# Four small memsets from GpSimd to VectorE, and one load from SyncE to ScalarE, at the start of an attention and gated FFN kernel

## The chip, the cores and the metric

The kernel runs on one core of a Trainium2 chip. The metric is the device time of one execution in microseconds (us), as the median of several executions. Engines are named as the profile names them: PE is TensorE (PEld its weight loads), DVE is VectorE, ACT is ScalarE, POOL is GpSimd, SP is SyncE. A load that GpSimd issues goes through DMA queue q0 (software_dynamic in the profile), one that SyncE or ScalarE issues through a hardware_dynamic queue (q1 for SyncE in this trace).

## The reference, cut to what matters

Attention over 8 batches with 8 heads, in which keys and values are first projected from 1024 positions to 64 by two small matrices E and F, followed by a gated feed-forward network over 8192 tokens.

```python
# q, k, v: (8, 8, 1024, 64); E, F: (64, 1024); w_gate, w_val: (512, 1536); w_out: (1536, 512)
k_proj = np.einsum('ks,bhsd->bhkd', E, k)
v_proj = np.einsum('ks,bhsd->bhkd', F, v)
scores = scale * np.matmul(q, k_proj.transpose(0, 1, 3, 2))
attn = softmax(scores)                       # written out in the reference
x = np.matmul(attn, v_proj)                  # -> (8192, 512) tokens
gate = 1.0 / (1.0 + np.exp(-(x @ w_gate)))
out = gate * (x @ w_val) @ w_out
```

So nothing can be projected before E, F and the first keys are on the chip, and nothing of the feed-forward network can start before a first block of attention is done.

## The kernel before: the parts that the change and the steps touch

The kernel is a list of operations; each is added with the keys it reads and writes, and waits between engines follow from these. Each engine runs its own operations in the order of the list. The parts that matter stand at its start.

```python
def pool(fn, r=(), w=()):
    return add("POOL", fn, r=r, w=w)

def load(o, i, w, sem, r=(), tie=()):        # every load of k, q, v and weights: issued by GpSimd
    add("POOL", lambda e: e.dma_start(o, i), r=r, w=w, dma=sem, t=26.0, tie=tie)

def start_loads():
    for src, rows, n in ((E, slice(0, 64), "E"), (F, slice(64, 128), "F")):
        add("SP", lambda e, src=src, rows=rows: e.dma_start(EF[rows, :], src[:, :]),
            w=[("EF", n)], dma="in" + n)
    for i in range(4):
        pool(lambda e, i=i: e.memset(quad[32 * i : 32 * i + 32, :], 32.0 * i), w=[("quad", i)])
    for R in range(2):
        load_kv_heads(0, k, R)               # keys of four heads, 512 KB
        load_q_half(0, 0, R)                 # queries of the same heads, half the tokens, 256 KB
    for R in range(2):
        load_kv_heads(1, v, R)               # values of four heads, 512 KB
    load_w(0, 0)                             # then weights, a column block at a time
    # ... more weights and the other half of the queries

def constants():                             # VectorE: builds identities and selectors
    dve(lambda e: e.memset(count[:, 0:1], 0.0), [], ["count"])
    # ... count = 0..127 along a row, by doubling (7 instructions), 4 patterns, one 32x32 transpose
    dve(lambda e: e.tensor_tensor(row_f[:, :], rows[:, 0, 0:1], quad[:, :], ALU.add),
        ["rows"] + [("quad", i) for i in range(4)], ["row_f"])
    # ... identf and ident = (count == row_f), then selectors

def project_consts():                        # TensorE: E and F transposed, with identf
    ev = EF[:, :].rearrange("k (p t) -> k t p", t=NT)
    for g in range(2):
        b = whole.next()
        for t in range(4):
            mm(b, bank[b][:, t * P : (t + 1) * P], ev[:, 4 * g + t, :], identf[:, :],
               [("EF", "E"), ("EF", "F"), "identf"], tr=True)
        act(EFT[:, 4 * g : 4 * g + 4, :].rearrange("p t c -> p (t c)"), bank[b][:, :],
            [], [("EFT", g)], b=b)           # ScalarE's first operation

# the program
start_loads()
blocks_ready(0)
constants()
project_consts()
busy(4)                                      # four matmuls on ident, results unused: fillers
qt, sc, den, bc, xo = half_unit(0, whole)
# ... then: project keys (waits for EFT and keys), transpose queries, scores, project values, ...
```

`quad` is a column of 128 numbers that holds 0, 32, 64 and 96 in its four groups of 32 partitions. It is read once, for `row_f`, the number of each partition, from which the identity matrices are made.

Of the kernel before, what the change touches and what calls it, by code (L numbers as in the profile page):

```python
# [237 lines left out]
def bass_linformer_attn__then__ffn_glu_sigmoid_kernel(  # L238
# [18 lines left out]
    with contextlib.ExitStack() as es:  # L257

        def sbuf(name, shape, dtype):
            return es.enter_context(nc.sbuf_tensor(name, shape, dtype))  # L260
# [8 lines left out]
        def within(shape, dtype):  # L269

            n = 1
            for x in shape[1:]:
                n *= x
            if dtype == FP32:
                n *= 2
            t = early[0][:, used[0] : used[0] + n]
            used[0] += n
            if dtype == FP32:
                t = t.bitcast(FP32)
            if len(shape) == 3:  # L280
                t = t.rearrange("p (a b) -> p a b", a=shape[1])
            if len(shape) == 4:
                t = t.rearrange("p (a b c) -> p a b c", a=shape[1], b=shape[2])
            return t
# [12 lines left out]
        rows = within([P, 4, 32], FP32)  # L297
        ident = within([P, P], BF16)
        quad = sbuf("quad", [P, 1], FP32)
# [91 lines left out]
        def dve(fn, r, w, b=None, t=None):  # L391
            x = [] if b is None else [("bank", b)]
            return add("DVE", fn, r=r, w=w, x=x, t=t)

        def pool(fn, r=(), w=()):
            return add("POOL", fn, r=r, w=w)
# [33 lines left out]
        def load_kv_heads(n, src, R):  # L430
            hh = slice(4 * R, 4 * R + 4)
            load(
                KV[n][:, hh, :],
                src[0].rearrange("h (p t) d -> p h (t d)", t=NT)[:, hh, :],
                [("KV", n, R)],
                f"KV{n}{R}",
            )
# [11 lines left out]
        def load_q_half(b, hf, R):  # L449
            cc, hh = slice(256 * hf, 256 * hf + 256), slice(4 * R, 4 * R + 4)  # L450
            load(
                Qb[:, hh, cc],
                q[b].rearrange("h (p t) d -> p h (t d)", t=NT)[:, hh, cc],
                [("Q", hf, R)],
                f"Q{hf}{R}",
            )
# [3 lines left out]
        def load_w(j, ih=None):  # L460
            c = slice(WCH[j], WCH[j + 1])
            ii = slice(0, NI) if ih is None else slice(2 * ih, 2 * ih + 2)
            for n, t, src in (("wG", wG, wg_v), ("wV", wV, wv_v)):
                load(
                    t[:, ii, c],
                    src[:, ii, c],
                    [(n, j, x) for x in ((0, 1) if ih is None else (ih,))],
                    f"{n}{j}" if ih is None else f"{n}{j}h{ih}",
                )


        def start_loads():
            for src, rows, n in ((E, slice(0, 64), "E"), (F, slice(64, 128), "F")):
                add(
                    "SP",
                    lambda e, src=src, rows=rows: e.dma_start(EF[rows, :], src[:, :]),
                    w=[("EF", n)],
                    dma="in" + n,
                )
            for i in range(4):  # L480
                pool(
                    lambda e, i=i: e.memset(quad[32 * i : 32 * i + 32, :], 32.0 * i),  # L482
                    w=[("quad", i)],
                )
            for R in range(2):
                load_kv_heads(0, k, R)
                load_q_half(0, 0, R)
            for R in range(2):
                load_kv_heads(1, v, R)
            load_w(0, 0)  # L490
            load_w(0, 1)
            load_w(1)
            load_w(2)
            for R in range(2):
                load_q_half(0, 1, R)
            load_w(3)
            load_w(4)
            load_w(5)

        def heads8():  # L500
            x = count[:, 0:8].rearrange("p (h b) -> p h b", h=2)
            return x.unsqueeze(2).to_broadcast([P, 2, 4, 4])

        def constants():
            dve(lambda e: e.memset(count[:, 0:1], 0.0), [], ["count"])
            for i in range(7):
                n = 1 << i
                dve(
                    lambda e, n=n: e.tensor_scalar(
                        count[:, n : 2 * n], count[:, 0:n], float(n), None, op0=ALU.add  # L510
                    ),
                    ["count"],
                    ["count"],
                )
            dve(lambda e: e.tensor_copy(pats[:, 0, :], count[:, 0:32]), ["count"], ["pats"])
            dve(
                lambda e: e.tensor_copy(
                    pats[:, 1, :].rearrange("p (h a b) -> p h a b", h=2, b=4),
                    heads8(),
                ),  # L520
                ["count"],
                ["pats"],
            )
            dve(
                lambda e: e.tensor_copy(
                    pats[:, 2, :].rearrange("p (a b) -> p a b", b=4),
                    count[:, 0:4].unsqueeze(1).to_broadcast([P, 8, 4]),
                ),
                ["count"],
                ["pats"],  # L530
            )
            dve(
                lambda e: e.tensor_scalar(
                    pats[:, 3, :].rearrange("p (a b) -> p a b", b=16),
                    count[:, 0:16].unsqueeze(1).to_broadcast([P, 2, 16]),
                    8.0,
                    -1.0,
                    op0=ALU.is_ge,
                    op1=ALU.mult,
                ),  # L540
                ["count"],
                ["pats"],
            )
            dve(
                lambda e: e.transpose(
                    rows[:, :, :].rearrange("p a b -> p (a b)"),
                    pats[:, :, :].rearrange("p a b -> p (a b)"),
                ),
                ["pats"],
                ["rows"],  # L550
            )
            dve(
                lambda e: e.tensor_tensor(row_f[:, :], rows[:, 0, 0:1], quad[:, :], ALU.add),
                ["rows"] + [("quad", i) for i in range(4)],
                ["row_f"],
            )
            for t, n in ((identf, "identf"), (ident, "ident")):
                dve(
                    lambda e, t=t: e.tensor_scalar(
                        t[:, :], count[:, :], row_f[:, 0:1], None, op0=ALU.is_equal  # L560
                    ),
                    ["count", "row_f"],
                    [n],
                )
            for n, op in ((0, ALU.is_ge), (1, ALU.is_lt)):
                dve(
                    lambda e, n=n, op=op: e.tensor_scalar(
                        half[:, n : n + 1], row_f[:, :], 64.0, None, op0=op
                    ),
                    ["row_f"],  # L570
                    [("half", n)],
                )
            for n in range(2):
                for i in range(4):
                    dve(
                        lambda e, n=n, i=i: e.tensor_scalar(
                            dsel8[:, n, i, :].rearrange("p (h a b) -> p h a b", h=2, b=4),
                            heads8(),
                            half[:, n : n + 1],
                            2.0 * i,  # L580
                            op0=ALU.subtract,
                            op1=ALU.is_equal,
                        ),
                        ["count", ("half", n)],
                        [("dsel8", n)],
                    )
            for t, k, m, i, v in (
                (bsel8f, "bsel8f", 8, 1, 0.25),
                (bsel8, "bsel8", 8, 1, 0.5),
            ):  # L590
                dve(
                    lambda e, t=t, m=m, i=i, v=v: e.tensor_scalar(
                        t[:, :, :, :].rearrange("p c h d -> p (c h) d"),
                        count[:, 0:m].unsqueeze(2).to_broadcast([P, m, 64]),
                        rows[:, i, 0:1],
                        v,
                        op0=ALU.is_equal,
                        op1=ALU.mult,
                    ),
                    ["count", "rows"],  # L600
                    [k],
                )
# [1462 lines left out]
        for b in range(1, B):  # L2065
            n = attention(b + 1) if b + 1 < B else None
# [61 lines left out]
```

The softmax here doesn't subtract the row's maximum and nothing guards it: scores larger than these inputs give would overflow.

## Time and profile before

Times before: 517.77 us as the median of 3 runs, 517.19 to 517.79. The profiled execution took 517.65 us, of which the profile spans 515.9 us from the first to the last instruction.

| quantity | value | where from |
|---|---|---|
| TensorE busy in 0 to 5 us, 5 to 10, 10 to 15, 15 to 20 | 0.00, 4.10, 4.37, 4.91 us | busy time by stretch |
| GpSimd busy in the same stretches | 4.25, 5.00, 5.00, 4.24 us | the same |
| memset of quad on GpSimd | 4, of 89 to 126 ns each | instructions of the tile quad |
| issue of E, issue of F on SyncE | 0.57 us each | instructions in order of time |
| time from issue to landing of E, of F | 3.7 us, 4.4 us | DMA issues |
| granted clock of TensorE | 1.000 | cores |

To read such a profile: a row of the timeline gives the start from the beginning of the span, the length, the engine, the line and operation, the tiles (a tile is named after the memory that it lies in: `count` and `identf` lie in vT, `ident` in gT), and in brackets how long the engine was idle before it and what ended that idle time. For a DMA, the row of the engine is the issue alone; the transfer runs later on the DMA engines. The chain of work is followed backwards from the last instruction: each piece is what released the next one.

### The profile page before, as it was taken

Reading aid. Unit: us, or ns where it says so; the run is one execution under the profiler, and the core shown is the slowest. Engines: PE = TensorE matmul, PEld = TensorE weight load, DVE = VectorE, ACT = ScalarE, POOL = GpSimd, SP = SyncE. Lnnn points to the kernel's source line nnn. Section 1 sums busy time; section 2 is a strip of 40 time slices with the busy share of each in tenths; the row PEclk is TensorE's granted clock in tenths of the full one; section 3 lists DMA queues with packets and bytes.
Section 4 is the critical chain, followed back from the end, with each engine's and each line's share of the span. In section 5 each row is a group of like instructions: output and inputs, shape, how many; then the busy total and the mean of one; then the engine's idle time right before and its main releaser. Section 6 shows DMA issues by size and latency. Waiting matters only on the chain.

```text
span 515.9 us, 11369 instructions
## 1 busy us (share of the span) xinstructions
PE 505.0 (98%) x4598; PEld 410.0 (79%) x4598; DVE 410.9 (80%) x809; ACT 345.0 (67%) x645; POOL 41.0 (8%) x60
## 2 busy tenths in 40 slices
PE   5999999999999999999999999999999999999996
PEld 3545645888888888888888888888888888888885
DVE  4548779899789796988879888797969898777774
ACT  2555683867778677677767776777676766676652
POOL 9420301200200020000100020000000000000000
PEclk9999999999999999999999999999999999999999
DMA  9999999899798788454946389374104330201013
GB/s 161 199 198 204 150 195 221 115 178 233 93 224 155 152 150 138 102 125 123 174 85 154 60 152 203 56 164 100 46 7 97 42 104 1 83 1 76 6 43 124
DMA packets 105205, 63.13 MB, mean 122 GB/s; under 512 B 63040, under 2 KB 97344, under 8 KB 105152
## 3 DMA queue, kind: packets, MB, share of 16 engines
q0 software_dynamic: 34000, 29.89, 37.5%
q1 hardware_dynamic: 71152, 32.52, 28.8%
q8 instruction: 36, 0.59, 0.4%
q14 instruction: 17, 0.14, 0.1%
HBM read 60.29 MB, written 16.78 MB: 149 GB/s over the span
## 4 chain that ended last, share of the span: by engine, by line
PE 94%; DMA 2%; DVE 1%; POOL 1%; issue 0%; ACT 0%; DVEq 0%; POOLq 0%
PE pA L385 51%; PE pF L385 43%; DMA KVs<-in_v_dram 2%; DVE hT L1832 0%; POOL KVs L403 0%; DVE vsnap L1710 0%; POOL Qb L403 0%; DVE xT L868 0%; DVE ost L1437 0%; ACT sig L389 0%; DVE sig L1786 0%; ACT vsnap L389 0%; DVE ost L1522 0%; POOL quad L482 0%; DVE hS L1382 0%
## 5 line engine op out<-in xcount | busy, mean ns | idle before, releaser
L389 ACT ACTIVATE sig<-pA 128x512 f32<-128x512 f32 x126 | 75.1, 596 | 43.4 <-PE pA L385 42.8
L1699 ACT ACTIVATE pF<-pA 128x512 f32<-128x512 f32 x99 | 58.5, 591 | 30.9 <-PE pA L385 26.3
L1710 DVE TENSOR_TENSOR vsnap<-pF,vsnap 128x512 f32<-128x512 f32 x90 | 61.8, 686 | 18.1 <-ACT vsnap L389 9.2
L1786 DVE TENSOR_TENSOR sig<-pF,sig 128x512 f32<-128x512 f32 x84 | 57.5, 685 | 7.2 <-PE pA L385 3.7
L385 PE MATMUL pF<-wO,hT 128*128 128x256 bf16 (+1 forms) x402 | 59.3, 285 | 0.0
L389 ACT ACTIVATE vsnap<-pA 128x512 f32<-128x512 f32 x84 | 50.2, 597 | 11.9 <-PE pA L385 11.8
L1832 DVE SCALAR_TENSOR_TENSOR hT<-sig,vsnap 128x512 bf16<-128x512 f32 x84 | 56.6, 683 | 0.9
L389 ACT ACTIVATE sig<-sig 128x512 f32<-128x512 f32 x84 | 52.8, 629 | 2.9 <-DVE sig L1786 2.6
L385 PE MATMUL pF<-xS,wV 128*128 128x256 bf16 x360 | 54.0, 273 | 0.1
L385 PE MATMUL pA<-xT,gT 128*128 128x256 bf16 x336 | 50.4, 273 | 0.0
L385 PE MATMUL pF<-xS,wG 128*128 128x256 bf16 x336 | 50.4, 273 | 0.0
L385 PE MATMUL pA<-xT,vT 128*128 128x256 bf16 x336 | 50.4, 273 | 0.0
L385 PE MATMUL pF<-xT,wG 128*128 128x256 bf16 (+1 forms) x264 | 50.2, 311 | 0.2 <-DVE xT L868 0.2
L389 ACT ACTIVATE sig<-pF 128x512 f32<-128x512 f32 x66 | 39.5, 598 | 15.0 <-PE pF L385 13.1
L385 PE MATMUL pA<-wT,hT 128*128 128x256 bf16 x360 | 48.8, 273 | 0.1
L1832 DVE SCALAR_TENSOR_TENSOR hT<-sig,pF 128x512 bf16<-128x512 f32 x42 | 28.7, 683 | 24.6 <-PE pF L385 24.4
L385 PEld LDWEIGHTS pF<-wO,hT 128*128 128x128 bf16 x402 | 38.7, 98 | 10.5 <-issue 0.8
L385 PE MATMUL pF<-xT,wV 128*128 128x256 bf16 (+1 forms) x240 | 41.5, 294 | 0.0
L385 PEld LDWEIGHTS pF<-xS,wV 128*128 128x128 bf16 x360 | 34.9, 98 | 6.1 <-DVE vsnap L1710 0.4
L385 PEld LDWEIGHTS pA<-wT,hT 128*128 128x128 bf16 x360 | 34.3, 98 | 5.6 <-ACT EF L389 0.8
L389 ACT ACTIVATE eT<-pA 128x512 bf16<-128x512 f32 x58 | 34.1, 596 | 5.7 <-PE pA L385 4.4
L385 PEld LDWEIGHTS pA<-xT,vT 128*128 128x128 bf16 x336 | 32.3, 98 | 5.2 <-issue 0.4
(159 smaller groups left out, 906.5 us busy)
## 6 DMA issues: line engine op xcount, KB each, us to landing
out_dram<-ost SPq DMA_DIRECT2D x61, 256.0 KB, 2.5
Qb<-in_q_dram POOLq DMA_DIRECT2D x7, 1024.0 KB, 11.9
KVs<-in_k_dram POOLq DMA_DIRECT2D x7, 1024.0 KB, 13.7
KVs<-in_v_dram POOLq DMA_DIRECT2D x7, 1024.0 KB, 18.0
wO<-in_moe_w_out_dram POOLq DMA_DIRECT2D x2, 768.0 KB, 9.8
wG<-in_moe_w_gate_dram POOLq DMA_DIRECT2D x5, 256.0 KB, 18.9
wV<-in_moe_w_val_dram POOLq DMA_DIRECT2D x5, 256.0 KB, 19.4
KVs<-in_k_dram POOLq DMA_DIRECT2D x2, 512.0 KB, 9.3
```

Of the source, the lines that this page charges most:

```text
L385: return add("PE", lambda e: e.matmul(o, lhsT, rhs, **kw), r=r, x=[("bank", b)])
L389: return add("ACT", lambda e: e.activation(o, i, func, scale=scale), r=r, w=w, x=x, t=t)
L1699: lambda e: e.activation(bank[c][:, :], bank[a][:, :], AF.Copy, scale=1.0),
L1710: lambda e: e.tensor_tensor(o, bank[bk][:, :], o, ALU.add),
L1786: dve(lambda e: e.tensor_tensor(o, bank[bk][:, :], o, ALU.add), [key], [key], b=bk)
L1832: lambda e: e.scalar_tensor_tensor(o, sg.rearrange("p (j c) -> p j c", j=2), 1.0, x.rearrange("p (j c) -> p j c", j=2), ALU.add, ALU.mult,),
```

## The change

Two things move. The four memsets of `quad` go from GpSimd, where they stand in front of the first load of keys, to VectorE, where they stand in front of the other constants. The load of F is issued by ScalarE and no longer by SyncE behind the load of E. The purpose is to let GpSimd issue its loads from its first instruction on, and to have E and F issued at the same time.

```diff
         def start_loads():
-            for src, rows, n in ((E, slice(0, 64), "E"), (F, slice(64, 128), "F")):
+            for eng, src, rows, n in (
+                ("SP", E, slice(0, 64), "E"),
+                ("ACT", F, slice(64, 128), "F"),
+            ):
                 add(
-                    "SP",
+                    eng,
                     lambda e, src=src, rows=rows: e.dma_start(EF[rows, :], src[:, :]),
                     w=[("EF", n)],
                     dma="in" + n,
                 )
-            for i in range(4):
-                pool(
-                    lambda e, i=i: e.memset(quad[32 * i : 32 * i + 32, :], 32.0 * i),
-                    w=[("quad", i)],
-                )
             for R in range(2):
                 load_kv_heads(0, k, R)
@@
         def constants():
+            for i in range(4):
+                dve(
+                    lambda e, i=i: e.memset(quad[32 * i : 32 * i + 32, :], 32.0 * i),
+                    [],
+                    [("quad", i)],
+                )
             dve(lambda e: e.memset(count[:, 0:1], 0.0), [], ["count"])
```

## The prediction

> **What bounds the kernel now.** I read the page first, then the chain of work that ended last for the first 60 us, then the instructions in order of time for the first 10 us, then the DMA rates in half-microsecond stretches. The page says that this is a TensorE kernel:
>
> ```profile
> PE 505.0 (98%) x4598; PEld 410.0 (79%) x4598; DVE 410.9 (80%) x809; ACT 345.0 (67%) x645; POOL 41.0 (8%) x60
> ...
> PE   5999999999999999999999999999999999999996
> ...
> PE 94%; DMA 2%; DVE 1%; POOL 1%; issue 0%; ACT 0%; DVEq 0%; POOLq 0%
> ```
>
> The reader should see two things. TensorE is the chain for 94% of the span, and only its first slice (13 us) has real holes. All that the change touches happens in the first 2.5 us, and it can act on the end only through those holes. So the gain cannot be more than a few microseconds out of 517.77, and the question is whether it is a half, nothing, or a loss. The chain of the start answers which wait ends last:
>
> ```profile
> 1.18 0.13 POOL quad L482
> 1.31 0.05 issue
> 1.36 0.89 POOL KVs L403
> 2.25 0.75 POOL Qb L403
> 3.00 0.74 POOL KVs L403
> 3.74 0.69 POOL Qb L403
> 4.43 12.83 DMA KVs<-in_v_dram
> ```
>
> Columns are start, length, piece. The four memsets of quad (the last of them is shown) stand in front of GpSimd's first load (keys, heads 0 to 3), the loads go out one behind the other, and the first load of values is issued fifth, at 4.43, and ends at 17.27 (4.43 + 12.83, rounded); the next piece is TensorE's, at 17.31, and from there the chain is nearly all TensorE. So the chain does lead through the memsets. But the fifth load took 12.83 us, which is a transfer in a queue, not an issue: whether the queue moves when its head is issued earlier has to be looked at. First the starts:
>
> ```profile
> 0.74 1.28 ACT L389 ACT_TABLE_LOAD   x1 [0.74 <-PEq L2113]
> 0.75 0.56 POOL L482 MEMSET quad<- 32x1 f32 x4 [0.29 <-POOLq L2113]
> 0.75 0.57 SPq L476 DMA_DIRECT2D EF<-in_E_dram  x1
> 0.82 0.06 DVE L505 MEMSET vT<- 128x1 f32 x1 [0.82 <-PEq L2113]
> 0.91 1.54 DVE L509 TENSOR_SCALAR vT<-vT 128x1 f32<-128x1 f32 x7
> 1.36 0.89 POOL L403 DMA_DIRECT2D KVs<-in_k_dram  x1
> 1.38 0.57 SPq L476 DMA_DIRECT2D EF<-in_F_dram  x1
> ...
> 5.86 1.94 PE L385 MATMUL pA<-vT,EF 128*128 128x128 f32 x8 [5.86 <-DMA EF<-in_F_dram]
> ```
>
> GpSimd spends 1.36 - 0.75 = 0.61 us on the memsets. SyncE issues E at 0.75 and F at 1.38, 0.63 us later, and TensorE's first work waits for F (5.86). The rates of DMA, last two columns share and GB/s:
>
> ```profile
> 2.00:2.50 0.50, 0.00 (x0) 0.00 (x0) 0.43 (x3) 0.03 (x1) 0.50 (x2) 1.00 1.06 131
> 2.50:3.00 0.50, 0.00 (x0) 0.00 (x0) 0.50 (x4) 0.00 (x0) 0.50 (x2) 1.00 0.69 270
> ...
> 4.00:4.50 0.50, 0.00 (x0) 0.00 (x0) 0.50 (x5) 0.00 (x0) 0.50 (x2) 1.00 0.84 150
> ```
>
> DMA starts at 2.3 us. In the trace's packet records E and F (q1) run from 2.34 to 5.06, and the first packet of GpSimd's queue (q0) starts only at 4.32, which is 2.96 us after its issue at 1.36. Loads that GpSimd issues into an empty queue later in the same trace start their first packet 1.8 us after issue (58.44 to 60.20, 98.25 to 100.07, 137.75 to 139.59, 183.81 to 185.63). So the first load is about 1.1 us later than its issue alone explains; the first completion packet of F is at 4.31. Either E and F stand before it on the engines, or the first use is slow.
>
> **What the Trainium skill says.** "DMA: Bandwidth & Descriptors", section "Issuing engines are not separate DMA queues", says that issuing from several engines only saves the issue time of the sequencer, since all run on the same 16 engines. The trace has that time: 0.57 us for one issue on SyncE. The same page, section "Queues, rings and completion order", says that a DMA engine takes turns between the queues it has work for, a packet at a time; the trace only partly agrees, as q0 starts when q1 is nearly done. "ScalarE: Activation LUTs", section "What ACT_TABLE_LOAD costs", gives about 1283 ns; the trace has 1.28 us, at ScalarE's very start, where the load of F is now to be issued. "SBUF — State Buffer", section "Who interferes with whom", says that a VectorE instruction with at most one SBUF input outside the two-port modes does not hold up GpSimd. A memset has no SBUF input, so the moved memsets should not disturb GpSimd's issues; no row of this trace isolates that.
>
> **The change part by part.** GpSimd loses four memsets: its first issue goes from 1.36 to about 0.75 to 0.80, so it gains 0.56 to 0.61 us, and so do the twenty or so issues behind it, as they follow back to back. They stay well ahead of the data: the fifth is issued at 4.43 and lands at 17.27.
>
> VectorE gains four memsets: one took 0.06 us and the next instruction started 0.09 us after it (0.82 to 0.91), so 4 x 0.09 = 0.36 us at most. It builds the identity for TensorE's first transposes: that instruction starts at 3.64, takes 0.29, and is done at 3.93. It becomes 4.29. TensorE waits for F until 5.86 (about 5.2 after the change), so about 0.9 us of slack remains. VectorE's constants end at 6.27 and its next work starts at 11.37. The cost is zero. One wait on GpSimd's semaphore disappears, too.
>
> SyncE's second issue goes to ScalarE. If ScalarE issues F in front of its table load, F goes out at 0.75, 0.63 us earlier; the table load then ends at about 2.6, long before ScalarE's first copy at 6.98. If the table load stays first, F is issued at 2.02, 0.64 us later than now. I take the first as more likely (0.75), because the load of the table belongs to the first activation and the issue stands ahead of that in the program.
>
> Now what of this reaches the end. Total work for the DMA engines up to the first values is unchanged: 0.5 MB of E and F, and 2.0 MB of keys, queries and values. What can be saved is engine time that is idle now. Between 2.34 and 3.0 the packet records show 26 packets of 4096 bytes start, 106 KB; at the rate of the next half microsecond (172 KB in 0.5 us) it would be 227 KB. The shortfall of about 120 KB is 0.35 us, because only E is there and its first packets are slow. With F issued beside E, and the keys 0.6 us earlier, that hole is filled: 0.35 us if the engines are simply first come, first served. If the delay of q0 is a fixed one after its issue, its head moves by the whole 0.56 to 0.61. I take the middle, 0.5 us. From the first q0 packet on the queue is full without a gap to 30 us, so keys (now 9.5), queries, second keys (13.46) and values (17.27) all move by that.
>
> TensorE can follow: it waits for the keys at 9.55, with fillers before them that end at about 9.5 and that move with F by 0.6; it waits 0.52 us for the second keys and 0.58 us for the values. Behind 17.31 it is one chain of TensorE work, and the shift goes through one for one: 517.77 - 0.5 = 517.27. I lean slightly lower, since one of the three times before was 517.19, and say 517.2.
>
> **The rivals.** (1) DMA-bound start: E and F fill the engines, so an earlier head of the keys only queues behind them. For it: q0 starts just when F's completions begin, share of DMA about 1. Against it: shares of 0.69 and 0.84 in the stretches shown. It gives 0 to 0.35 us, 517.4 to 517.8. (2) The table load stays ahead of F: F lands at about 6.4, TensorE's transposes and fillers end 0.6 us later (10.1), so the keys no longer bind. But its idle time before the second keys and values, 0.52 + 0.58 = 1.1 us, absorbs that, and the values still come earlier; the gain would be 0.3 to 0.6, 517.2 to 517.5. (3) VectorE becomes the bound, if a memset cost far more than 0.09 us: it would need over 0.2 us each to pass F. Unlikely; it would give at most the time before. (4) Everything shifts but later loads, transposes by DMA and TensorE meet in another order, worth some tenths either way. That is the spread of the three times before, 0.6 us.
>
> **Range and chances.** The mechanism gives 0 to 0.6 us of gain, so 517.17 to 517.77; the spread of 0.3 us either way around that gives 516.6 to 517.9 as the range. 2% is 10.4 us: nothing here is of that size, neither removed nor added. Faster by over 2%: 0.005; within 2%: 0.985; slower by over 2%: 0.01.
>
> **What would show it.** Right: first load of keys issued at about 0.75 to 0.8; F issued by ScalarE at about 0.75, first TensorE transpose at about 5.2 instead of 5.86; identity done at about 4.3; first projection of keys at about 9.0 instead of 9.55; the wait for the values ends at about 16.8 instead of 17.31; all later stretches equal in length. Wrong: values still at 17.3 although keys are issued earlier (rival 1); the F issue behind the table load (rival 2); TensorE's first wait put down to VectorE (rival 3); or the gain present at 17 us and gone later, by a wait that is not there now.

## The result and the profile after

The changed kernel takes 533.3 us (median, 532.68 to 533.73) against 517.76 for the kernel before (517.19 to 518.9). The ratio is 1.0298, with a 95% interval of 1.0285 to 1.0311: 15.5 us slower. The prediction said 517.2, at most 517.9.

The page of the changed kernel, with the rows that were shown of before (busy time, TensorE in 40 slices of 13.3 us, chain by engine):

```profile
PE 505.1 (95%) x4598; PEld 410.3 (77%) x4598; DVE 410.8 (77%) x813; ACT 345.1 (65%) x645; POOL 40.0 (8%) x56
...
PE   0399999999999999999999999999999999999997
...
PE 94%; POOL 3%; DVE 2%; issue 0%; ACT 0%; DVEq 0%; POOLq 0%
```

TensorE has as much to do as before (505.1 us against 505.0), but its first slice now reads 0 and its second 3, where it had 5 and 9. So nothing became more costly; TensorE begins late. In the chain, GpSimd's share grows from 1% to 3%, which is about 16 us. The instructions of the changed kernel in order of time say when each engine begins (start, length, engine, operation, and in brackets the idle time before it with what ended it):

```profile
0.75 0.55 ACTq L479 DMA_DIRECT2D EF<-in_F_dram  x1
0.75 0.58 SPq L479 DMA_DIRECT2D EF<-in_E_dram  x1
1.25 0.89 POOL L403 DMA_DIRECT2D KVs<-in_k_dram  x1 [0.80 <-POOLq L2117]
1.33 1.28 ACT L389 ACT_TABLE_LOAD   x1 [1.33 <-PEq L2117]
...
16.63 0.92 POOL L403 DMA_DIRECT2D wV<-in_moe_w_val_dram  x1
17.36 1.15 POOL L918 MEMSET kpd<- 128x1024 bf16 x1
18.56 0.40 DVE L505 MEMSET quad<- 32x1 f32 x4 [18.56 <-POOL kpd L918]
19.02 0.06 DVE L509 MEMSET vT<- 128x1 f32 x1
...
22.02 1.94 PE L385 MATMUL pA<-vT,EF 128*128 128x128 f32 x8 [22.02 <-DVE vT L563]
```

What the change set out to move has moved: F is issued by ScalarE at 0.75, ahead of the table load, and GpSimd has no memsets in front of its loads. But VectorE's first instruction, the first moved memset, starts at 18.56 instead of 0.82, and the bracket names what it waited for: `POOL kpd L918`, a memset of the tile kpd that GpSimd reaches only behind all 22 of its load issues. The waits of the first 24 us, by engine, line, what was waited for, then total, times and longest:

```profile
PE pA L385 <- DVE vT L563: 22.0, 1, 22.0
...
DVE quad L505 <- POOL kpd L918: 18.6, 1, 18.6
```

And the chain of the changed kernel at this place (start, length, piece):

```profile
16.07 0.74 POOL wG L403
16.81 0.74 POOL wV L403
17.55 0.97 POOL kpd L918
21.04 0.32 DVE gT L549
21.59 0.30 DVE vT L563
22.02 1.94 PE pA L385 x8
```

The rates of DMA, in the same stretches as shown of before (last two columns share and GB/s):

```profile
2.00:2.50 0.50, 0.00 (x0) 0.00 (x0) 0.00 (x0) 0.50 (x1) 0.50 (x2) 1.00 0.21 82
2.50:3.00 0.50, 0.00 (x0) 0.00 (x0) 0.00 (x0) 0.11 (x1) 0.50 (x2) 1.00 0.91 319
...
4.00:4.50 0.50, 0.00 (x0) 0.00 (x0) 0.00 (x0) 0.00 (x0) 0.50 (x2) 1.00 0.97 160
```

The weak stretch from 2.5 to 3.0 (0.69) is better filled, at 0.91, but 2.0 to 2.5 is emptier; nothing in the transfers accounts for 15 us.

The chain no longer leads through the transfer of the values. It runs along GpSimd's issues, through the clearing of kpd, through VectorE's constants to the identity, and into TensorE.

How the 15.5 us add up, from the two timelines. These rows give the identity and the first projection of values, in the kernel before:

```profile
3.64 0.29 DVE L559 TENSOR_SCALAR vT<-vT,row_f 128x128 f32<-128x128 f32 x1
...
17.31 0.48 PEld L385 LDWEIGHTS pA<-KVs,EFT 128*64 128x64 bf16 x16 [0.58 <-DMA KVs<-in_v_dram]
```

and in the changed kernel:

```profile
21.59 0.29 DVE L563 TENSOR_SCALAR vT<-vT,row_f 128x128 f32<-128x128 f32 x1
...
32.78 0.48 PEld L385 LDWEIGHTS pA<-KVs,EFT 128*64 128x64 bf16 x16 [0.42 <-issue]
```

VectorE starts 18.56 - 0.82 = 17.7 us later; the identity is done at 21.88 instead of 3.93, 17.95 later; 1.93 of it had been slack before F landed (3.93 to 5.86), so TensorE starts 22.02 - 5.86 = 16.16 later; TensorE's later waits for keys and values vanish, since all of that has landed by then: the first projection of values starts at 32.78 instead of 17.31, 15.47 later; and the span ends 531.5 - 515.9 = 15.6 later. All of the loss is made before TensorE's first instruction.

Where the wait comes from is in two places of the code that the diff does not touch:

```python
def blocks_ready(n):
    if n == 0:      # GpSimd clears kpd, and declares that it READS quad
        pool(lambda e: e.memset(kpd[:, :, :, :], 0.0), [("quad", i) for i in range(4)],
             [("kpd", 0), ("kpd", 1), "preset"])
        return

# Plan.add: an operation that writes a key waits for every reader listed since the key's last write
for k in tuple(w) + tuple(x):
    for o in self.writers.get(k, ()):
        dep(o, False)
    for o in self.readers.get(k, ()):
        dep(o, False)
```

The clearing does not use quad. In the kernel before, the declaration made GpSimd wait for its own four memsets, which were long done. The program lists start_loads, then blocks_ready(0), then constants. As the memsets moved from start_loads to constants, they moved past the clearing: a write of quad now stands behind a reader of quad on another engine, so VectorE must wait for it, and that engine issues 22 loads first.

### The profile page after: what moved, and what is told of

It reads as the page before. It is cut to its first block, busy times and chain, and to the rows that moved or that the text cites. A ratio compares the mean times of both kernels' runs of the same rounds, so it can differ in the third digit from the quotient of the medians.

```text
span 531.5 us, 11368 instructions
## 1 busy us (share of the span) xinstructions
PE 505.1 (95%) x4598; PEld 410.3 (77%) x4598; DVE 410.8 (77%) x813; ACT 345.1 (65%) x645; POOL 40.0 (8%) x56
## 4 chain that ended last, share of the span: by engine, by line
PE 94%; POOL 3%; DVE 2%; issue 0%; ACT 0%; DVEq 0%; POOLq 0%
PE pA L385 51%; PE pF L385 43%; POOL wG L403 1%; POOL wV L403 1%; POOL KVs L403 1%; POOL Qb L403 1%; DVE hT L1836 0%; DVE vsnap L1714 0%; DVE vT L513 0%; POOL kpd L918 0%; DVE xT L872 0%; DVE ost L1441 0%; ACT sig L389 0%; DVE sig L1790 0%; ACT vsnap L389 0%
## 6 DMA issues: line engine op xcount, KB each, us to landing
wO<-in_moe_w_out_dram POOLq DMA_DIRECT2D x2, 768.0 KB, 10.5
```

## The experiments

Theory W is the wait just described. Rival P: the ports; VectorE's memset is held up physically by GpSimd's own work. Rival Q: the second issuing engine costs. The kernel before, run beside the experiments, took 517.5 us beside "the reading struck", "the wait alone", "the load of F alone" and "the memsets alone", and 517.86 beside the other four.

**The reading struck.** The change as it is, and one word of it taken out elsewhere:

```diff
-pool(lambda e: e.memset(kpd[...], 0.0), [("quad", i) for i in range(4)], [("kpd", 0), ("kpd", 1), "preset"])
+pool(lambda e: e.memset(kpd[...], 0.0), [], [("kpd", 0), ("kpd", 1), "preset"])
```

> The change whole, but GpSimd's clearing of kpd no longer declares that it reads quad. Theory W (a wait): VectorE's first memset stood behind that clearing only because the clearing is listed before it as a reader of quad; without the reading VectorE starts at about 0.8 us, the identity is done at about 4.3, TensorE starts when E lands, at about 5.5 instead of 5.86, and the time is 517.3 to 517.8 us. Rival P (a port): VectorE's memset is held up physically by GpSimd's work on its own loads or memset; then VectorE still starts at about 18.5 and the time stays at 533. Rival Q (the second issuing engine costs): part of the 15.5 us stays.

Measured: 517.17 us, ratio to before 0.9993 (0.9985 to 1.0002). The whole loss is gone. In the timeline of this kernel:

```profile
0.75 0.57 SPq L479 DMA_DIRECT2D EF<-in_E_dram  x1
0.75 0.57 ACTq L479 DMA_DIRECT2D EF<-in_F_dram  x1
0.81 0.40 DVE L505 MEMSET quad<- 32x1 f32 x4 [0.81 <-PEq L2117]
1.26 0.89 POOL L403 DMA_DIRECT2D KVs<-in_k_dram  x1 [0.80 <-POOLq L2117]
...
4.28 0.29 DVE L563 TENSOR_SCALAR vT<-vT,row_f 128x128 f32<-128x128 f32 x1
...
5.76 1.95 PE L385 MATMUL pA<-vT,EF 128*128 128x128 f32 x8 [5.76 <-DMA EF<-in_F_dram]
```

VectorE starts at 0.81 and works on beside GpSimd's issues from 1.26, and its identity is done at 4.57; nothing physical holds it until 18.5, so P falls. (The four memsets end at 1.21, ahead of the first issue; in the two doses below they run beside issues.) TensorE's first work starts at 5.76, not at the 5.5 that was expected: it still waits for F. The time lies 0.1 us under the expected range, which was counted from 517.76.

**The order alone.** The changed kernel with the reading kept and two lines of the program swapped:

```diff
 start_loads()
-blocks_ready(0)
 constants()
+blocks_ready(0)
```

> The changed kernel with two lines of the program swapped: the constants are listed before the clearing of kpd, which keeps its reading of quad. Theory W: the order in the list alone decides who waits for whom; now GpSimd's clearing waits for VectorE's memsets, which are done at about 1.3 us, long before GpSimd comes to it at 17. VectorE starts at 0.8, and the time is 516.7 to 517.8 us, as with the reading struck. If striking the reading had helped in some other way, this one would stay near 533.

Measured: 517.25 us, ratio 0.9986 (0.9977 to 0.9995). The same instructions, with GpSimd waiting for VectorE and not the reverse, are as fast as with the reading struck: VectorE starts at 0.81, TensorE at 5.70, and the clearing comes at 17.93. The order in the list decides who waits.

**The wait alone.** The kernel before, with nothing of the change, but one declared reading added to VectorE's first instruction:

```diff
-dve(lambda e: e.memset(count[:, 0:1], 0.0), [], ["count"])
+dve(lambda e: e.memset(count[:, 0:1], 0.0), [("kpd", 0)], ["count"])
```

> The kernel before, with one thing added: VectorE's first memset (count) declares that it reads kpd and so waits for GpSimd's clearing of it. All else is as before: the four memsets on GpSimd, E and F on SyncE. Theory W: this wait alone makes the whole loss; VectorE starts at about 18.7 us (0.1 later than in the changed kernel, as GpSimd's first load is 0.11 later), TensorE at about 21.7, and the time is 532.5 to 533.7 us. Rivals P and Q: what was lost came with the moved memsets or the moved load, and the time is near 518.

Measured: 532.48 us, ratio 1.0293 (1.0280 to 1.0307), against 1.0298 for the change. From its list of instructions that touch quad and from its waits:

```profile
L482 POOL MEMSET quad<- x4: 89/92/94, 0.7 to 1.2; 32x1 f32 x4
```

```profile
DVE vT L505 <- POOL kpd L914: 18.8, 1, 18.8
```

The memsets are on GpSimd at 0.7 to 1.2 us, E and F on SyncE, and the loss is there; TensorE starts at 21.75, as expected. Nothing else of the change is needed for it.

**The load of F alone** (the kernel before, F issued by ScalarE, memsets on GpSimd).

```diff
-for src, rows, n in ((E, slice(0, 64), "E"), (F, slice(64, 128), "F")):
-    add("SP", ...)
+for eng, src, rows, n in (("SP", E, slice(0, 64), "E"), ("ACT", F, slice(64, 128), "F")):
+    add(eng, ...)
```

> The kernel before, with only the load of F moved to ScalarE; the memsets stay on GpSimd. Theory W: no wait arises, TensorE starts at about 5.5, where E lands beside F, 0.3 us earlier than before, of which 0 to 0.3 reach the end: 517.4 to 517.9 us. Rival Q: the load from ScalarE costs, and the time is well over 518. Rival P says nothing of it.

Measured: 517.02 us, ratio 0.9990 (0.9981 to 1.0000). Q falls. The expected start of TensorE at 5.5 fell as well:

```profile
0.75 0.56 ACTq L479 DMA_DIRECT2D EF<-in_F_dram  x1
...
0.75 0.58 SPq L479 DMA_DIRECT2D EF<-in_E_dram  x1
...
5.92 1.57 PEld L385 LDWEIGHTS pA<-vT,EF 128*128 128x128 f32 x8 [5.92 <-DMA EF<-in_E_dram]
5.92 1.97 PE L385 MATMUL pA<-vT,EF 128*128 128x128 f32 x8 [5.92 <-DVE vT L595]
```

Both loads are issued at 0.75 and TensorE starts at 5.92, as late as before. The weight load names what it waited for: E, which landed 5.1 us after its issue, at 5.88. (The bracket of the first matmul names a selector that VectorE had just finished, the last event before the start; TensorE's operands don't come from it, and the identity was done at 3.94.) The packet records tell how E came to be late: F's packets run from 2.11 to 3.81, and E's begin at 3.19 and end at 4.87. In the version with the reading struck it is the other way round, E from 2.11 to 3.65 and F from 3.13 to 4.78. Issued together, the two queues are served nearly one after the other, and the second to come ends where F ended before (4.82). Issuing F 0.6 us earlier did not start TensorE earlier. (The time lies under the expected range, which was counted from 517.76; the kernel before ran at 517.5 beside these, so the ratio is what counts, here and in the next.)

**The memsets alone** (the kernel before, memsets on VectorE, reading struck, F on SyncE; the second half of the diff of the change and the strike above).

> The kernel before, with only the memsets of quad moved to VectorE and the reading of quad struck from the clearing of kpd; F stays on SyncE. Theory W: VectorE starts at 0.8, GpSimd's first load goes out at about 1.25 instead of 1.36, TensorE starts at 5.8 with F, and the time is 517.5 to 517.9 us. Rival P: VectorE waits for GpSimd, and the time is 533.

Measured: 517.26 us, ratio 0.9999 (0.9991 to 1.0008). No gain and no loss; TensorE starts at 5.68.

**Two doses of the wait.** The changed kernel, its wait kept, with the clearing of kpd moved up in GpSimd's list, to behind 6 and behind 14 of the 22 loads:

```diff
             for R in range(2):
                 load_kv_heads(1, v, R)
+            blocks_ready(0)          # first dose; second dose: behind load_w(2)
...
 start_loads()
-blocks_ready(0)
 constants()
```

> The changed kernel with the clearing of kpd moved up in GpSimd's list to behind its six loads of keys, queries and values (in the changed kernel it stands behind 22 loads). VectorE still waits for it. Theory W: the clearing ends at about 6.9 us (four issues of 0.74 and two more end at 5.8, and the clearing takes 1.15), VectorE starts at 6.95, needs 3.3 us to the identity (18.56 to 21.88 in the changed kernel), so TensorE starts at 10.3 instead of 5.86; 0.5 of the 4.4 us are absorbed by waits for keys and values that vanish, as in the changed kernel: 521.0 to 521.9 us.

> As the last, with the clearing behind fourteen of the 22 loads. Theory W: it starts at 11.5 us, where the fifteenth load is issued in the changed kernel, and ends at 12.65; VectorE starts at 12.7 and TensorE at 16.0 to 16.2, 10.2 later than before, less 0.5: 526.8 to 527.8 us. The three places then lie on one line: each issue ahead of the clearing costs about 0.7 us of the whole time.

Measured: 522.46 us (ratio 1.0081, 1.0064 to 1.0097) and 528.39 (1.0198, 1.0182 to 1.0214). Behind 6, 14 and 22 loads the loss is 4.6, 10.5 and 15.5 us: 5.9 for the first eight issues more, 5.0 for the next eight, some 0.7 us for each issue that the clearing waits behind. VectorE itself starts at 6.87, 12.66 and 18.56, 5.8 and 5.9 apart. The place in GpSimd's queue sets the loss. Both times are 0.5 to 0.6 us above the expected ranges, and the timeline of the first dose shows where:

```profile
5.80 1.01 POOL L919 MEMSET kpd<- 128x1024 bf16 x1
...
6.87 0.40 DVE L506 MEMSET quad<- 32x1 f32 x4 [6.87 <-POOL kpd L919]
...
9.79 0.52 DVE L530 COPY vT<-vT 128x32 f32<-128x32 f32 x1
9.88 0.46 DVE L538 TENSOR_SCALAR vT<-vT 128x32 f32<-128x32 f32 x1
...
10.91 0.29 DVE L564 TENSOR_SCALAR vT<-vT,row_f 128x128 f32<-128x128 f32 x1
...
11.34 1.94 PE L385 MATMUL pA<-vT,EF 128*128 128x128 f32 x8 [11.34 <-DVE vT L564]
```

VectorE starts at 6.87, as expected, but needs 11.20 - 6.87 = 4.33 us to the identity and not 3.32 as in the changed kernel (4.52 in the second dose). That is taken up in the last section.

**The start of GpSimd's first load.** The version with the reading struck, two memsets of quad on each engine:

> The version with the reading struck, but two of the four memsets of quad stay on GpSimd, in front of its first load (the clearing reads those two). Only the start of the first load of keys is asked for: it began at 1.36 with four memsets in front and at 1.26 with none. If something else holds GpSimd's first load until about 1.26, then two memsets in front leave it at 1.25 to 1.27; if the memsets cost it in proportion, it begins at about 1.31. The time is 516.7 to 517.8 us either way.

```profile
1.31 0.89 POOL L403 DMA_DIRECT2D KVs<-in_k_dram  x1 [0.33 <-issue]
```

The first load begins at 1.31 (one run, 518.48 us, from which nothing is concluded): this is what was expected if the memsets cost in proportion. With no memset, two and four in front it begins at 1.26, 1.31 and 1.36. So the start moves in proportion to their number, but by only 0.1 us in all, while four memsets took 0.56 us of GpSimd. The bracket after the two memsets is 0.33 us of idle time put down to "issue", and with no memset GpSimd is idle until 1.26, where the other engines begin at 0.75 to 0.81: most of the memsets' time lay in a gap that is there anyway. What fills the gap, the runs do not show.

## Why the prediction was wrong, by its own steps

**The step that failed** is the second part of "the change part by part": VectorE gains four memsets, "the cost is zero", and one wait on GpSimd's semaphore disappears. The size of the memsets was about right: with the reading struck, VectorE's next instruction starts 0.46 us after the first of them (0.81 to 1.27) where 0.36 was said, and the identity, done at 4.57, is still 1.2 us ahead of TensorE's start. What it left out is that the moved writes get new neighbours in the list. It looked at who reads quad for its value, row_f, and not at who declares it. The operation between the old and the new place is the clearing, in a helper of the unchanged code. The wait that disappeared was replaced by one on the same semaphore, ahead of everything that VectorE does; striking it gives 517.17, adding it to the kernel before gives 532.48.

The list of what would show the prediction wrong had the right sign, TensorE's first wait put down to VectorE, but tied it to the cost of a memset (rival 3), and so gave it no weight.

**GpSimd's first issue** was to go from 1.36 to 0.75 or 0.80. It went to 1.25. The term of 0.61 us was mis-sized: only 0.11 of it lies on the path to the first load.

**F from ScalarE** went out at 0.75 with the table load behind it, as predicted. That TensorE then starts at 5.2 was wrong: without the wait it starts at 5.76, or at 5.92 with F alone moved. It needs both loads, and the one served second lands at 5.67 (F) or 5.88 (E), where F landed at 5.76 before.

**The head of the keys' queue.** The prediction took the middle between a head that moves by 0.6 and one that stays behind E and F. It does not follow the issue: the first packet of q0 is at 4.10 with the reading struck, at 4.11 with F alone moved, and at 4.08 before; over all ten traces it lies between 3.88 and 4.40, in no order of the issue. Rival 1 was right on that point. Yet with the reading struck the keys are used at 9.16 instead of 9.55, and the values at 16.80 instead of 17.31; in the chain with the reading struck their load is issued at 4.34 and ends at 16.76 (4.43 and 17.27 before):

```profile
4.34 12.42 DMA KVs<-in_v_dram
```

That this is the predicted 16.8 may be luck. The first values land between 15.48 and 17.23 in the six traces with GpSimd's first load at 1.25 or 1.26, and between 16.91 and 17.27 in the other four. These are single profiles, and whether the queue moves faster behind the same head, and why, was not tried.

**Readings and sums.** The packet times in the prediction lie 0.24 us too high against the timeline: E and F run from 2.10 to 4.82 and q0 starts at 4.08. The rate row of 2.0 to 2.5 shows it: 131 GB/s are 16 packets of 4096 bytes, and by the prediction's times only 10 would have started by 2.5. Loads into an empty queue then start 1.5 to 1.6 us after issue, not 1.8; the 1.1 us by which the first load comes later stay as they were, since the same 0.24 is in both. A spread of 0.3 us around 517.17 to 517.77 gives 516.9 to 518.1, not 516.6 to 517.9. In rival 3 a memset would have to cost 0.32 us to reach the predicted start of TensorE ((5.2 - 3.93) / 4), not 0.2. None of this bears on the loss.

**The intended gain** was put at 0.5 us. With the wait gone, the change gives 517.17 and 517.25 us in its two forms, ratios 0.9993 and 0.9986, that is 0.4 and 0.7 us, of which the first can't be told from nothing. The number 517.2 would have been right for the change that was meant, but by luck: of the terms behind it, 0.61 us for GpSimd measured 0.11, and 0.63 for F moved TensorE's start by less than 0.2 (5.76, 5.70 and 5.92, after 5.86 before).

## What to carry to other kernels

Before an operation is moved to another engine, look up every earlier reader and writer of what it writes, declared ones too, between the old place and the new. Where waits follow from the order of a list, a write that passes a reader on another engine turns into a wait for that engine, and on an engine that issues loads this means a wait for all the issues ahead of it. If the first instruction of an engine has a wait in its bracket, look there first: here it cost 15.5 us, where the change was for half a microsecond.

## What the runs showed of the hardware that was not expected

GpSimd's issues and some of VectorE's operations hold each other up. Copies of 128x32 float32 on VectorE, with GpSimd done with its issues (the changed kernel) and beside them (the kernel with the second dose):

```profile
20.57 0.18 DVE L519 COPY vT<-vT 128x32 f32<-128x32 f32 x1
20.67 0.17 DVE L521 COPY vT<-vT 128x32 f32<-128x32 f32 x1
20.75 0.17 DVE L529 COPY vT<-vT 128x32 f32<-128x32 f32 x1
```

```profile
15.78 0.48 DVE L520 COPY vT<-vT 128x32 f32<-128x32 f32 x1
15.87 0.41 DVE L522 COPY vT<-vT 128x32 f32<-128x32 f32 x1
15.96 0.34 DVE L530 COPY vT<-vT 128x32 f32<-128x32 f32 x1
```

The same copies take 0.17 to 0.18 us alone and 0.34 to 0.48 beside the issue that starts at 15.36 and takes 0.89. They are held rather than slowed: they end at 16.26, 16.28 and 16.30, and the issue at 16.25. Not every part of an issue does this: in the first dose, copies that started 0.13 and 0.22 us after an issue (9.62 and 9.71 after 9.49) took 0.18 and 0.17, and one that started 0.30 after it was held until 10.31, where that issue ends. In the other direction, with the reading struck, the issue at 5.80 takes 1.26 us beside VectorE's two operations on 128x512 float32 (6.04 and 6.43), and 0.76 in the changed kernel at 5.79, where VectorE stands still. The Trainium skill has this in "SBUF — State Buffer", section "Who interferes with whom": VectorE in its two-port modes (copy and tensor_scalar can enter them) and GpSimd lock each other out of a shared pair of ports. The numbers agree with that, and it would explain why both doses came out over their ranges: there VectorE builds its constants beside issues. Other operations show nothing of it: the four memsets, which have no input there, take 59 ns each at 0.8 us in the version with the order swapped and 59 ns beside issues in the first dose, and the 128x128 transpose takes 0.31 us alone and 0.31 beside the issue at 16.10 in the second.

The same skill, in "DMA: Bandwidth & Descriptors", section "Queues, rings and completion order", says that an engine takes turns between its queues a packet at a time, a packet being typically 9 to 17 descriptors. For E and F from two queues, issued within 0.01 us of each other, the runs show turns of nearly a whole load: the second queue's first record comes 1.0 to 1.1 us after the first one's (3.13 after 2.11, 3.19 after 2.11), when 51 and 58 of the first load's 64 data records have started. This need not contradict the page: by an estimate, 64 records on 16 engines are 4 for each, which one such packet could hold. The records do not name the engine, so that is not shown.
